# Token blocks of the later experts turned by VectorE instead of TensorE

## The chip, the cores and the metric

The kernel runs on one core of one Trainium2 chip. The metric is the device time of one execution in microseconds. A core has TensorE (matmuls, PE in the profile; its weight loads are PEld), VectorE (DVE), ScalarE (ACT), GpSimd (POOL), SyncE (SP, which here only issues DMAs) and 16 DMA engines. Each engine works through its own instructions in the order in which they were written; engines wait for each other by semaphores.

## The reference

A gated linear attention over 4 batches of 768 tokens with 8 heads of 48 gives 3072 rows `x` of 384 numbers. A router then picks one expert of eight per token, and each expert is a two-layer network:

```python
logits = x @ w_gate
e_idx = np.argmax(logits, axis=1)
...
for e in range(E):
    mask = e_idx == e
    h = np.maximum(x[mask] @ w1[e], 0.0)
    ye = h @ w2[e]
    out[mask] = gate_w[mask, None] * eom[mask, e, None] * ye
```

`w1[e]` is 384 by 1024 and `w2[e]` 1024 by 384, all in float32.

## The kernel before, in words

**Attention and sorting.** The first part of the program computes the attention and scatters every token's row into a DRAM buffer `xs_dram`. A row has 401 floats (1604 bytes): 384 of `x`, the number of the token, 8 logits and 8 output-gate logits. Each expert has its own stretch of that buffer, so after the scatter the tokens of one expert lie one behind the other.

**Experts.** The experts are then taken in order of their number of tokens; `s` counts them from 0 and has room for `CAPS` = 512, 448, 432, 416, 400, 400, 384, 376 tokens. Every product is made of three matmuls on a high and a low part of each operand (`xh`, `xl`, `w1h`, `w1l` and so on), which ScalarE and VectorE split: ScalarE rounds (`nc.scalar.copy`), VectorE subtracts. A stage of an expert has two halves. `mm1` (L750) multiplies `w1` with the tokens, eight blocks `f` of 128 rows of `h`, three chunks `c` of 128 features each, nine matmuls a block. `mm2` (L773, and `mm2_rows`, L787, for the last two experts, which have three row tiles) multiplies `w2` with `h`.

**Where the tokens come in.** `mm1` needs the tokens with their features on the partitions, but they lie in DRAM with one token to a row. `tokens_in` (L655) loads them in tiles `xg` of 128 tokens by 401 floats with one DMA. `x_in` (L721) turns them: for each chunk `c`, TensorE transposes three or four tiles of up to 128 tokens by 128 features into the PSUM tile `x_ps` (L711), then ScalarE casts `x_ps` to `xh` (L717) and VectorE subtracts it to get `xl` (L718).

**The order around it.** All orders are written out by hand. During the `mm2` half of stage `s`, a list `front` holds four splits of the next expert's `w1` (L636, L637) and three calls of `x_in(s + 1, c)` (L891 to L896). One entry is taken at each `f` of `mm2` (L907), or at every third step of `mm2_rows` (L900); the small operations that make the output gain of the next expert (`gain_ops`, L681) are taken in between. They are appended to each engine's instruction list behind the matmuls of that `f`. The last entry of `front` is `x_in(s + 1, 2)`; after it come the copies of the finished `y_ps` (`y_out`, L804), and then the first `mm1` of the next stage. TensorE also turns the finished output back (`put`, L811).

**The loads.** SP issues for each next expert four loads of `w1r` (L614), then the tokens (L658), then four of `w2r` (L626). The buffers of `w1r` and `w2r` are free again when a split has read them, so SP waits for the splits. Expert 0 is special: its tokens come in two parts into `first_x`, and are turned by TensorE in `x_early` and `x_late`.

Of the kernel before, what the change touches and what calls it, by code (L numbers as in the profile page):

```python
# [8 lines left out]
F32 = mybir.dt.float32  # L9
# [11 lines left out]
N, DM, E, F = B * S, H * D, 8, 1024  # L21
# [3 lines left out]
CAPS = (512, 448, 432, 416, 400, 400, 384, 376)  # L25
WARM = 22
TS = 128
NT = 4
SLOTS = NT * TS
WIDE = max(CAPS[1:])  # L30
# [4 lines left out]
KC = DM // 128  # L35
# [5 lines left out]
LG = DM + 1  # L41
RW = LG + 2 * E
RG = (4, 4, 4, 4, 2, 2, 2, 2)
XW = 2 * D + 2 * E
T_SCAT = 8
HELD = 256


class Consts:
# [66 lines left out]
class Routing:  # L116


    def __init__(self, pool):
        self.pend = pool.tile([128, NTC * NP], F32, name="pend")  # L120

        self.ohb = pool.tile([128, len(RG) + 1, 5, E], BF16, name="ohb")
        self.slot = pool.tile([128, NTC], I32, name="slot")
        self.top = pool.tile([128, E], F32, name="top")
        self.top_id = pool.tile([128, 1], I32, name="top_id")


def attention(ctx, tc, nc, k, kpool, rt, q01, k01, f01, q23, k23, f23, v, wg, xs_dram, r, ex):
# [205 lines left out]
    def scatter(n):  # L334

        for _ in range(min(n, len(sq))):
# [6 lines left out]

            for other in ex.apart + (ex.cleared if (t + 1) * C <= HELD else []):
                tc.declare_no_dep(i.ins, other.ins, reason="other slots")
# [77 lines left out]
    last = len(order) - 1  # L423
    pre_of = [prep(t) for t in range(len(order))]
    load(0, [("fqk", 0, 2), ("f", 2, 4), ("v", 0, 2), ("qk", 2, 4)])
    nc.sync.dma_start(out=turn[:, 0::2, 2 * D:XW], in_=wg[:, 0::2, 0:2 * E])
    for i in range(2):
        nc.sync.dma_start(out=turn[64 * i:64 * i + 64, 1::2, 2 * D:XW],
                          in_=wg[64 - 64 * i:128 - 64 * i, 1::2, 0:2 * E])
    load(0, [("v", 2, 4), ("fkqv", 4, 6)])  # L430
    load(1, [("fkqv", 0, 2), ("fkqv", 2, 4), ("fkqv", 4, 6)])
    for e in range(E):
        ex.clear(e)
# [144 lines left out]
class Experts:  # L578
# [4 lines left out]
    def __init__(self, tc, nc, k, r, raw, right, w1, w2, xs_dram, out, kp):  # L583
        self.tc, self.nc, self.k, self.r, self.raw, self.right, self.kp = tc, nc, k, r, raw, right, kp
        self.w1, self.w2, self.xs, self.out = w1, w2, xs_dram.rearrange("(e n) w -> e n w", e=E), out
        k.gain = kp.tile([TS, NT, E], F32, name="gain")
        k.dst = kp.tile([TS, NT, E], I32, name="dst")

        self.first = kp.tile([TS, NT, RW], F32, name="first_x")
        self.apart, self.cleared, self.number = [], [], {}  # L590
        self.wr, self.whl, self.todo, self.gq = {}, {}, [], []
        self.xg, self.xt, self.hs, self.ys, self.ysb = {}, {}, {}, {}, {}

    def open_early(self):
        pool = lambda name, bufs: self.right.enter_context(
# [14 lines left out]
    def load(self, s, number, rest=True):  # L610
        e = self.number[s] = self.nc.values_load(number, engines=[mybir.EngineType.SP], min_val=0, max_val=E - 1)
        for i in range(KF // 2):
            t = self.raw.tile([128, KC, 256], F32, name="w1r")
            self.nc.sync.dma_start(out=t, in_=self.w1[bass.ds(e, 1), :, 256 * i:256 * i + 256].rearrange(  # L614
                "o (c p) f -> p (o c) f", p=128))
            self.wr[1, s, i] = t
        if rest:
            self.load_rest(s)

    def load_rest(self, s):  # L620
        e = self.number[s]
        if s > 0:
            self.tokens_in(s, 0, len(self.rows(s)))
        for i in range(KF // 2):
            t = self.raw.tile([128, 2, DM], F32, name="w2r")
            self.nc.sync.dma_start(out=t, in_=self.w2[bass.ds(e, 1), 256 * i:256 * i + 256].rearrange(  # L626
                "o (c p) d -> p (o c) d", p=128))
            self.wr[2, s, i] = t
# [15 lines left out]
    def clear(self, e):  # L644

        if e == 0:
            self.empty = self.kp.tile([TS, RW], F32, name="empty")
            self.nc.gpsimd.memset(self.empty, 0.0)
            self.nc.gpsimd.memset(self.empty[:, DM:DM + 1], float(BIG))
        n = (SLOTS - HELD) // TS  # L650
        i = self.nc.sync.dma_start(out=self.xs[e, HELD:SLOTS].rearrange("(j p) w -> p j w", p=TS),
                                   in_=self.empty.unsqueeze(1).broadcast_to([TS, n, RW]))
        self.cleared.append(i)

    def tokens_in(self, s, j0, j1):  # L655
        early = s == 0 and j0 == 0
        t = self.first[:, j0:j1] if s == 0 else self.xp.tile([TS, NT, RW], F32, name="xg")
        i = self.nc.sync.dma_start(  # L658
            out=t[:, 0:j1 - j0, :],
            in_=self.xs[bass.ds(self.number[s], 1), j0 * TS:j1 * TS].rearrange("o (j p) w -> p (o j) w", p=TS))  # L660
        if early:

            for other in self.apart[T_TOP:]:
                self.tc.declare_no_dep(i.ins, other.ins, reason="other slots")
            self.apart.append(i)
        for j in range(j0, j1):
            self.xg[s, j] = (t[:, j - j0, :], min(TS, CAPS[s] - j * TS))
        if not early:
            self.meta = getattr(self, "meta", []) + [(s, 0, j1, t if s > 0 else self.first)]

    def gains(self):

# [8 lines left out]
    def gain_ops(self, s, j0, j1, t, d, up, dn, mx, sm, so):  # L681
        nc, k = self.nc, self.k
        tt, red, act = nc.vector.tensor_tensor, nc.vector.tensor_reduce, nc.scalar.activation
        sig, n = AF.Sigmoid, j1 - j0
        lg, og = t[:, 0:n, LG:LG + E], t[:, 0:n, LG + E:RW]
        mine = k.perm[:, s, :] if s > 0 else self.r.top
        return [
            lambda: nc.gpsimd.tensor_scalar(out=k.dst[:, j0:j1, s], in0=t[:, 0:n, DM], scalar1=0.0,
                                            scalar2=float(BIG), op0=ALU.max, op1=ALU.min),
            lambda: red(out=mx, in_=lg, axis=AX.X, op=ALU.max),  # L690
            lambda: tt(out=d, in0=lg, in1=mx.unsqueeze(2).broadcast_to([128, n, E]), op=ALU.subtract),

            lambda: (act(out=up, in_=d, func=sig), act(out=dn, in_=d, func=sig, scale=-1.0)),
            lambda: tt(out=d, in0=og, in1=mine.unsqueeze(1).broadcast_to([128, n, E]), op=ALU.mult),
            lambda: red(out=so, in_=d, axis=AX.X, op=ALU.add),
            lambda: act(out=so, in_=so, func=sig),
            lambda: nc.vector.reciprocal(out=dn, in_=dn),
            lambda: tt(out=up, in0=up, in1=dn, op=ALU.mult),
            lambda: red(out=sm, in_=up, axis=AX.X, op=ALU.add),
            lambda: nc.vector.tensor_scalar(out=sm, in0=sm, scalar1=1e-9, scalar2=None, op0=ALU.add),  # L700
            lambda: nc.vector.reciprocal(out=sm, in_=sm),
            lambda: tt(out=k.gain[:, j0:j1, s], in0=sm, in1=so, op=ALU.mult),
        ]
# [15 lines left out]
        return hi[:, 0:n], lo[:, 0:n]  # L719

    def x_in(self, s, c):  # L721
        ps = self.psx.tile([128, 512], F32, name="x_ps")
        for j, _ in self.rows(s):
            self.x_tr(s, c, ps, j, j * TS)
        self.xt[s, c] = self.x_split(self.xp, c, ps[:, 0:CAPS[s]], CAPS[s], WIDE, "x")

    def x_early(self):
        ps2 = self.psx.tile([128, 512], F32, name="x_ps")
# [189 lines left out]
def check(nc, k, r, pool, psum):  # L918
# [13 lines left out]
    def verdict():  # L932
        with nc.allow_low_precision(reason="a count of at most 17"):
# [7 lines left out]
        lambda: nc.vector.tensor_tensor(out=bad[:, 1:1 + E], in0=k.tokens, in1=k.caps, op=ALU.is_gt),  # L941
        lambda: nc.vector.tensor_scalar(out=bad[:, 1 + E:1 + 2 * E], in0=k.tokens, scalar1=float(HELD), scalar2=None,
                                        op0=ALU.is_lt),
# [189 lines left out]
```

## Time and profile before

| | |
|---|---|
| median of 3 runs | 380.4 us (378.98 to 382.08) |
| profiled execution | 383.17 us, its span 381.4 us |
| PE busy | 363.3 us, 95% of the span |
| DVE busy | 234.7 us, 62% |
| ACT busy | 197.7 us, 52% |
| POOL busy | 145.8 us, 38% |
| mean granted TensorE clock | 0.998 of full speed |

Times in the profile are microseconds from the start of the span. The attention takes the first 135 us or so; stages 0 to 7 follow, and the last matmul starts at 375.04. A busy share is an average over stages, so the rows below are read stage by stage.

### The profile page before, as it was taken

The page shows a single profiled execution, that of the slowest core. Times are in us where ns is not written, and L with a number is a line of the kernel's source. Part 1 is how long each engine was busy: PE and PEld are TensorE (multiplying, and loading weights), DVE is VectorE, ACT ScalarE, POOL GpSimd, SP SyncE. Part 2 cuts the span into 40 slices and gives each one's busy share as a digit, 9 for nine tenths or more (in the row PEclk, how much of TensorE's full clock was granted, in tenths as well). Part 3 has the DMA queues.
Part 4 walks back from the last instruction along what each step waited for, and adds up shares of the span by engine and source line. Part 5 has one row for each costly group of instructions (what it writes and reads, how often), then busy time and mean ns, then how long its engine had stood idle before and what let it go on. Part 6 is the DMA issues. An engine that isn't in the chain of part 4 may idle for free. (4 is left out here: it accounts for less than half of the span.)

```text
span 381.4 us, 8425 instructions
## 1 busy us (share of the span) xinstructions
PE 363.3 (95%) x3199; PEld 334.6 (88%) x3199; DVE 234.7 (62%) x482; ACT 197.7 (52%) x468; POOL 145.8 (38%) x176
## 2 busy tenths in 40 slices
PE   7899999998979999999999999999999999999993
PEld 2688978897868899989989999999999999999993
DVE  6988979897994773655644545463554554554610
ACT  3576856865745641536525634543652653753510
POOL 6686787997968670002201210310220220233012
PEclk9999999999999999999999999999999999999999
DMA  8999999999139327853434353445354354331001
GB/s 262 350 358 358 310 245 247 290 274 281 47 108 306 137 93 235 306 170 123 148 99 171 137 171 128 158 158 169 125 188 147 125 177 157 124 101 42 16 23 41
DMA packets 49315, 67.75 MB, mean 178 GB/s; under 512 B 3682, under 2 KB 43893, under 8 KB 49264
## 3 DMA queue, kind: packets, MB, share of 16 engines
q1 hardware_dynamic: 45952, 57.46, 49.6%
q0 software_dynamic: 3312, 9.65, 7.0%
q8 instruction: 27, 0.44, 0.5%
q14 instruction: 24, 0.20, 0.2%
HBM read 54.16 MB, written 13.39 MB: 177 GB/s over the span
## 5 line engine op out<-in xcount | busy, mean ns | idle before, releaser
L822 POOL DMA_INDIRECT out<-o,dst x30 | 30.2, 1007 | 188.3 <-ACT o L817 102.6
L766 DVE SCALAR_TENSOR_TENSOR hl<-h_ps,hh 128x256 fp32r<-128x256 f32 (+6 forms) x72 | 39.3, 546 | 53.1 <-ACT hh L765 52.3
L761 PE MATMUL h_ps<-xh,w1h 128*128 128x400 f32 (+6 forms) x192 | 67.3, 351 | 0.3 <-DVE hl L766 0.3
L761 PE MATMUL h_ps<-xh,w1l 128*128 128x400 f32 (+6 forms) x192 | 65.0, 338 | 0.0
L761 PE MATMUL h_ps<-xl,w1h 128*128 128x400 f32 (+6 forms) x192 | 64.9, 338 | 0.0
L765 ACT ACTIVATE hh<-h_ps 128x256 fp32r<-128x256 f32 (+6 forms) x72 | 34.8, 484 | 50.3 <-PE h_ps L761 48.6
L783 PE MATMUL y_ps<-hh,w2h 128*128 128x256 f32 (+4 forms) x168 | 57.7, 343 | 0.0
L783 PE MATMUL y_ps<-hl,w2h 128*128 128x256 f32 (+4 forms) x168 | 55.7, 332 | 0.0
L783 PE MATMUL y_ps<-hh,w2l 128*128 128x256 f32 (+4 forms) x168 | 55.6, 331 | 0.0
L718 DVE TENSOR_TENSOR xl<-x_ps,xh 128x400 fp32r<-128x400 f32 (+6 forms) x23 | 13.1, 568 | 41.8 <-ACT xh L717 38.5
L761 PEld LDWEIGHTS h_ps<-xh,w1h 128*128 128x128 f32 x192 | 36.1, 188 | 1.2 <-DVE hl L766 0.5
L761 PEld LDWEIGHTS h_ps<-xl,w1h 128*128 128x128 f32 x192 | 36.2, 188 | 0.4
L761 PEld LDWEIGHTS h_ps<-xh,w1l 128*128 128x128 f32 x192 | 36.0, 188 | 0.5
L717 ACT CAST xh<-x_ps 128x400 fp32r<-128x400 f32 (+6 forms) x23 | 11.3, 490 | 48.5 <-PE x_ps L711 42.4
L224 POOL TENSOR_TENSOR q_t<-q_t,p 128x512 f32<-128x512 f32 x24 | 30.6, 1276 | 9.6 <-DVE p L210 8.0
L637 DVE TENSOR_TENSOR w2l<-w2r,w2h 128x768 fp32r<-128x768 f32 x31 | 30.7, 991 | 4.2 <-ACT w2h L636 1.3
L783 PEld LDWEIGHTS y_ps<-hh,w2h 128*128 128x128 f32 x168 | 31.6, 188 | 1.0
L783 PEld LDWEIGHTS y_ps<-hl,w2h 128*128 128x128 f32 x168 | 31.6, 188 | 0.5
L783 PEld LDWEIGHTS y_ps<-hh,w2l 128*128 128x128 f32 x168 | 31.7, 188 | 0.4
L246 PE MATMUL a_ps<-q_t,k_t 64*128 64x128 f32 x384 | 28.3, 285 | 3.3 <-DVE k_t L221 2.7
L210 DVE TENSOR_TENSOR_SCAN p<-f_ps,start_p 128x511 f32<-128x511 f32 x22 | 28.0, 1273 | 3.9 <-ACT start_p L198 2.2
L323 PE MATMUL x_ps<-turn,xt 128*128 128x112 f32 x192 | 26.2, 280 | 3.8 <-ACT xt L317 3.6
(175 smaller groups left out, 773.1 us busy)
## 6 DMA issues: line engine op xcount, KB each, us to landing
w1r<-in_w SPq DMA_DIRECT2D x32, 384.0 KB
w2r<-in_w SPq DMA_DIRECT2D x32, 384.0 KB
xg<-xs_dram SPq DMA_DIRECT2D x5, 802.0 KB
xs_dram<-empty SPq DMA_DIRECT2D x8, 401.0 KB
f_t<-in_f SPq DMA_DIRECT2D x6, 512.0 KB
q_t<-in_q SPq DMA_DIRECT2D x6, 512.0 KB
k_t<-in_k SPq DMA_DIRECT2D x6, 512.0 KB
v_t<-in_v SPq DMA_DIRECT2D x6, 512.0 KB
```

Source lines behind the costliest of these rows:

```text
L210: nc.vector.tensor_tensor_scan(out=flat(d["p"])[:, 1:n], data0=flat(d["f"])[:, 0:n - 1], data1=sp[:, 1:n], initial=sp[:, 0:1], op0=ALU.mul ...
L224: nc.gpsimd.tensor_tensor(out=q_t[i][:, :, sl], in0=q_t[i][:, :, sl], in1=d["p"], op=ALU.mult)
L246: nc.tensor.matmul(aps[t][par][:, g, :], k_t[b % 2][r, g, sl], q_t[b % 2][r, g, sl], start=(g == 0), stop=(g == NP - 1))
L323: nc.tensor.matmul(xps[t][:, g, :], xt[t][:, g, :], turn[:, g, :], start=(g == 0), stop=(g == NP - 1))
L637: (eng or self.nc.vector).tensor_tensor(out=flat(lo), in0=flat(t), in1=flat(hi.bitcast(F32)), op=ALU.subtract)
L717: self.nc.scalar.copy(out=hi[:, 0:n], in_=ps)
L718: self.nc.vector.tensor_tensor(out=lo[:, 0:n], in0=ps, in1=hi.bitcast(F32)[:, 0:n], op=ALU.subtract)
L761: nc.tensor.matmul(ps[:, 0:n], a[:, c, cs], b, start=(i == 0), stop=(i == 3 * KC - 1))
L765: nc.scalar.activation(out=hi, in_=ps[:, 0:n], func=AF.Relu)
L766: nc.vector.scalar_tensor_tensor(out=lo, in0=ps[:, 0:n], scalar=0.0, in1=hi.bitcast(F32), op0=ALU.max, op1=ALU.subtract)
L783: self.nc.tensor.matmul(self.ys[d][:, c0:c0 + n], a[:, f % 2, ds], b, start=(f == 0 and i == 0 and part == 0), stop=(f == KF - 1 and i == ...
L822: self.nc.gpsimd.indirect_dma_start(out=self.out, out_offset=bass.IndirectOffsetOnAxis(ap=self.k.dst[0:n, j, s:s + 1], axis=0), in_=t[0:n] ...
```

## The change

For the experts 1 to 7 the tokens are no longer loaded as rows of 401 floats. Four DMAs each bring 96 of the 384 features of every token into one group of 32 partitions: token `32 a + t` lies on partition `32 b + t`, block `a`, where `b` is the group. A fifth DMA brings the token's number and the logits (`xm`). VectorE's transpose turns every 32 by 32 square of a tile in one instruction; with every third of the 96 features taken (`c::KC`), partition `32 b + i` then holds feature `96 b + 3 i + c`, which is `3 p + c` for partition `p`. The rows of `w1` are loaded in that same order. ScalarE's cast and VectorE's subtraction read the new SBUF tile `xc` in place of `x_ps`. Expert 0 is loaded and turned as before.

```diff
+SB = 32
+BW = DM // (128 // SB)
...
             self.nc.sync.dma_start(out=t, in_=self.w1[bass.ds(e, 1), :, 256 * i:256 * i + 256].rearrange(
-                "o (c p) f -> p (o c) f", p=128))
+                "o (p c) f -> p (o c) f" if s > 0 else "o (c p) f -> p (o c) f", p=128))
...
         if s > 0:
-            self.tokens_in(s, 0, len(self.rows(s)))
+            self.blocks_in(s)
...
+    def blocks_in(self, s):
+
+        e, nb, nt = self.number[s], -(-CAPS[s] // SB), len(self.rows(s))
+        t = self.xp.tile([128, SLOTS // SB, BW], F32, name="xb")
+        for b in range(128 // SB):
+            self.nc.sync.dma_start(
+                out=t[SB * b:SB * b + SB, 0:nb, :],
+                in_=self.xs[bass.ds(e, 1), 0:nb * SB, BW * b:BW * b + BW].rearrange("o (a t) w -> t (o a) w", t=SB))
+        m = self.xp.tile([TS, NT, RW - DM], F32, name="xm")
+        self.nc.sync.dma_start(
+            out=m[:, 0:nt, :],
+            in_=self.xs[bass.ds(e, 1), 0:nt * TS, DM:RW].rearrange("o (j p) w -> p (o j) w", p=TS))
+        self.xb[s] = t[:, 0:nb, :]
+        self.meta = getattr(self, "meta", []) + [(s, 0, nt, m)]
...
     def x_in(self, s, c):
-        ps = self.psx.tile([128, 512], F32, name="x_ps")
-        for j, _ in self.rows(s):
-            self.x_tr(s, c, ps, j, j * TS)
-        self.xt[s, c] = self.x_split(self.xp, c, ps[:, 0:CAPS[s]], CAPS[s], WIDE, "x")
+
+        t = self.xb[s]
+        n = t.shape[1] * SB
+        x = self.xp.tile([128, SLOTS], F32, name="xc")
+        self.nc.vector.transpose(out=x[:, 0:n].rearrange("p (a t) -> p a t", t=SB), in_=t[:, :, c::KC])
+        self.xt[s, c] = self.x_split(self.xp, c, x[:, 0:CAPS[s]], CAPS[s], WIDE, "x")
```

`gain_ops` reads the number and the logits from `xm` (or from the tail of `first_x` for expert 0) in place of `xg`.

## Rows read from the trace of the kernel before

**Rows 1.** The page's first part: busy time, share of the span and instructions of an engine.

```profile
PE 363.3 (95%) x3199; PEld 334.6 (88%) x3199; DVE 234.7 (62%) x482; ACT 197.7 (52%) x468; POOL 145.8 (38%) x176
```

**Rows 2.** Busy time by stretch: from and to, length, then busy time and number of instructions of PE, PEld, DVE, ACT and POOL, the granted TensorE clock, the mean busy share of the DMA engines, and GB/s. The first stretch lies in stage 0, the second is most of stage 1.

```profile
146.00:156.00 10.00, 10.00 (x84) 9.83 (x84) 4.33 (x13) 4.00 (x12) 0.79 (x2) 1.00 0.95 318
170.00:202.00 32.00, 32.00 (x168) 28.91 (x168) 16.60 (x37) 15.32 (x29) 4.49 (x5) 1.00 0.39 128
```

**Rows 3.** Everything that PE's matmuls waited for between 136 and 381 us: who waited for whom, us in total, times, the longest.

```profile
PE h_ps L761 <- DVE hl L766: 0.3, 1, 0.3
PE x_ps L711 <- DVE xl L718: 0.2, 1, 0.2
```

**Rows 4.** The instructions that read the tile `xg`: the transposes on PE, with their durations (least, median, greatest, ns), first and last start.

```profile
L711 PE MATMUL x_ps<-ident,xg x78: 230/272/327, 161.0 to 348.0; 128*128 128x128 f32 x60, 16*128 16x16 f32 x6, 64*128 64x64 f32 x3, 48*128 48x48 f32 x3
```

**Rows 5.** PE in order of time around one call of `x_in`, in the `mm2` half of stage 1: start, duration, instruction. Matmuls overlap, so starts are compared.

```profile
190.73 0.36 PE L783 MATMUL y_ps<-hh,w2l 128*128 128x448 f32 x1
190.93 0.36 PE L783 MATMUL y_ps<-hl,w2h 128*128 128x448 f32 x1
191.13 0.68 PE L711 MATMUL x_ps<-ident,xg 128*128 128x128 f32 x4
...
192.26 0.37 PE L783 MATMUL y_ps<-hl,w2h 128*128 128x448 f32 x1
```

**Rows 6.** The same around a call in stage 3.

```profile
253.49 0.35 PE L783 MATMUL y_ps<-hl,w2h 128*128 128x416 f32 x1
...
254.75 0.35 PE L783 MATMUL y_ps<-hl,w2h 128*128 128x416 f32 x1
254.94 0.35 PE L783 MATMUL y_ps<-hh,w2h 128*128 128x416 f32 x1
```

**Rows 7.** The same around a call in stage 6, where three tiles are turned.

```profile
340.38 0.34 PE L797 MATMUL y_ps<-w2h,hl 128*128 128x384 f32 x1
340.55 0.34 PE L797 MATMUL y_ps<-w2l,hh 128*128 128x384 f32 x1
340.73 0.48 PE L711 MATMUL x_ps<-ident,xg 128*128 128x128 f32 x3
...
341.41 0.34 PE L797 MATMUL y_ps<-w2l,hh 128*128 128x384 f32 x1
```

**Rows 8.** The same around the third call in stage 0.

```profile
165.36 0.28 PE L783 MATMUL y_ps<-hh,w2l 128*128 128x256 f32 x1
165.48 0.28 PE L783 MATMUL y_ps<-hl,w2h 128*128 128x256 f32 x1
165.98 0.75 PE L711 MATMUL x_ps<-ident,xg 128*128 128x128 f32 x4 [0.22 <-DVE xl L718]
...
167.00 0.28 PE L783 MATMUL y_ps<-hl,w2h 128*128 128x256 f32 x1
```

**Rows 9.** DVE's and ACT's groups by line and shape: count, busy us in total, mean ns of one, idle time before.

```profile
L718 DVE TENSOR_TENSOR xl<-x_ps,xh 128x448 fp32r<-128x448 f32 x3 | 1.9, 621 | 2.2 <-ACT xh L717 2.2
L718 DVE TENSOR_TENSOR xl<-x_ps,xh 128x256 fp32r<-128x256 f32 x2 | 0.8, 424 | 3.7 <-DMA w1r<-in_w 3.3 <-ACT xh L717 0.4
L210 DVE TENSOR_TENSOR_SCAN p<-f_ps,start_p 128x511 f32<-128x511 f32 x22 | 28.0, 1273 | 3.9 <-ACT start_p L198 2.2 <-ACT xt L317 0.9 <-ACT f_ps L205 0.7
L717 ACT CAST xh<-x_ps 128x448 fp32r<-128x448 f32 x3 | 1.6, 535 | 3.1 <-PE x_ps L711 3.1
```

**Rows 10.** DVE in order of time through the `mm2` half of stage 0, which has the tokens of stage 1 to turn, and ACT's last split there.

```profile
160.18 0.96 DVE L637 TENSOR_TENSOR w1l<-w1r,w1h 128x768 fp32r<-128x768 f32 x1 [0.30 <-ACT w1h L636]
161.06 0.18 DVE L690 TENSOR_REDUCE g_mx<-xg 128x4 f32<-128x32 f32 x1
...
163.26 0.82 ACT L636 CAST w1h<-w1r 128x768 fp32r<-128x768 f32 x1
...
167.33 0.62 DVE L718 TENSOR_TENSOR xl<-x_ps,xh 128x448 fp32r<-128x448 f32 x1 [1.15 <-ACT xh L717]
```

**Rows 11.** PE's first matmul of the next stage's `mm1`: after stage 0, after stage 1, and after stage 6.

```profile
169.94 0.37 PE L761 MATMUL h_ps<-xh,w1h 128*128 128x448 f32 x1
202.50 0.36 PE L761 MATMUL h_ps<-xh,w1h 128*128 128x432 f32 x1
350.18 0.34 PE L761 MATMUL h_ps<-xh,w1h 128*128 128x376 f32 x1
```

**Rows 12.** DVE in stage 1: the second of four splits of `w1`. Then ACT's copy of the second output tile of stage 6.

```profile
188.31 0.95 DVE L637 TENSOR_TENSOR w1l<-w1r,w1h 128x768 fp32r<-128x768 f32 x1
345.87 0.58 ACT L801 ACTIVATE o<-y_ps,gain 128x384 f32<-128x384 f32 x1 [0.64 <-PE y_ps L797]
```

**Rows 13.** The tokens' way in, in order of time: SP's issue for stage 1 and the instruction on POOL that waited for its landing; SP's issue for stage 3 and the first transposes of those tokens.

```profile
148.62 0.37 SPq L658 DMA_DIRECT2D xg<-xs_dram  x1
155.47 0.88 POOL L688 TENSOR_SCALAR dst<-xg 128x4 int32<-128x4 f32 x1 [8.93 <-DMA xg<-xs_dram]
199.26 0.37 SPq L658 DMA_DIRECT2D xg<-xs_dram  x1
223.01 0.66 PE L711 MATMUL x_ps<-ident,xg 128*128 128x128 f32 x4
```

**Rows 14.** The page's third part: a DMA queue with its packets, MB, and the time of the packets as a share of 16 engines' span.

```profile
q1 hardware_dynamic: 45952, 57.46, 49.6%
q0 software_dynamic: 3312, 9.65, 7.0%
```

More of the change, by code (lines that the diff above doesn't have):

```diff
@@ L591, in __init__ @@
         self.wr, self.whl, self.todo, self.gq = {}, {}, [], []
-        self.xg, self.xt, self.hs, self.ys, self.ysb = {}, {}, {}, {}, {}
+        self.xg, self.xb, self.xt, self.hs, self.ys, self.ysb = {}, {}, {}, {}, {}, {}
     def open_early(self):
@@ L655, in tokens_in @@
     def tokens_in(self, s, j0, j1):
-        early = s == 0 and j0 == 0
-        t = self.first[:, j0:j1] if s == 0 else self.xp.tile([TS, NT, RW], F32, name="xg")
+        early = j0 == 0
+        t = self.first[:, j0:j1]
         i = self.nc.sync.dma_start(
-            out=t[:, 0:j1 - j0, :],
-            in_=self.xs[bass.ds(self.number[s], 1), j0 * TS:j1 * TS].rearrange("o (j p) w -> p (o j) w", p=TS))
+            out=t, in_=self.xs[bass.ds(self.number[s], 1), j0 * TS:j1 * TS].rearrange("o (j p) w -> p (o j) w", p=TS))
         if early:
@@ L668, in tokens_in @@
         if not early:
-            self.meta = getattr(self, "meta", []) + [(s, 0, j1, t if s > 0 else self.first)]
+            self.meta = getattr(self, "meta", []) + [(s, 0, j1, self.first[:, :, DM:RW])]
+    def blocks_in(self, s):
[11 more added lines that the diff above has]
+        self.meta = getattr(self, "meta", []) + [(s, 0, nt, m)]
     def gains(self):
@@ L684, in gain_ops @@
         sig, n = AF.Sigmoid, j1 - j0
-        lg, og = t[:, 0:n, LG:LG + E], t[:, 0:n, LG + E:RW]
+        lg, og = t[:, 0:n, 1:1 + E], t[:, 0:n, 1 + E:1 + 2 * E]
         mine = k.perm[:, s, :] if s > 0 else self.r.top
         return [
-            lambda: nc.gpsimd.tensor_scalar(out=k.dst[:, j0:j1, s], in0=t[:, 0:n, DM], scalar1=0.0,
+            lambda: nc.gpsimd.tensor_scalar(out=k.dst[:, j0:j1, s], in0=t[:, 0:n, 0], scalar1=0.0,
                                             scalar2=float(BIG), op0=ALU.max, op1=ALU.min),
```

## The prediction

> **What bounds the kernel now.** I began with the page's first part: PE is busy for 95% of the span, and no other engine for more than 62% [rows 1]. A busy share doesn't yet say that PE sets the pace, so I went on to busy time by stretch. In stage 1 PE is busy for all 32.00 us, while DVE has 16.60 and ACT 15.32 [rows 2]. The list of waits then says the same from the other side: between 136 and 381 us the matmuls waited 0.5 us in all for anybody [rows 3]. So from about 139 us to the end the time is the sum of what PE's queue holds, and an instruction taken out of that queue is worth what it costs there, as long as nothing else comes late in its place.
>
> **What is taken out of PE's queue.** 78 transposes [rows 4], in 21 calls of `x_in`: 15 calls of four tiles (experts 1 to 5), 6 of three (experts 6 and 7). Their durations overlap with the matmuls around them, so I price a call by starts: from the last matmul before it to the third after it, less three ordinary steps. In stage 1: 192.26 - 190.93 = 1.33, less 3 x 0.20, is 0.73 [rows 5]. In stage 3: 1.26 less 3 x 0.19 is 0.69 [rows 6]. With three tiles: 0.86 less 3 x 0.175 is 0.33 [rows 7]. In stage 0 the matmuls are 0.12 apart, and the third call, which also waits for DVE to free `x_ps`, costs 1.52 - 0.36 = 1.16 [rows 8]; for the other two I take 0.72. Sum: 12 x 0.71 + 6 x 0.33 + (2 x 0.72 + 1.16) = 8.5 + 2.0 + 2.6 = **13.1 us**.
>
> **What VectorE gets.** 21 transposes, each of up to 448 elements on 128 partitions. No row shows such an instruction. The nearest ones by size: a subtraction of 448 takes 0.62, one of 256 takes 0.42, a scan of 511 takes 1.27 [rows 9]. The least I allow is 0.42 (a pass at almost two elements in the time of one), the most 1.27 (a pass as slow as the scan's); I take 0.62, since the transpose too reads and writes each element once, as the subtraction does and the scan, which carries a result along, does not. Cast and subtraction now read SBUF; I leave them at 0.54 and 0.62 [rows 9]. DVE's busy time grows by 3 x 0.62 = 1.9 us in a stage of 30, from half busy. That is no bound. What counts is the order: transpose, cast on ACT, subtraction follow each other, some 1.9 us a chunk with the handovers, and DVE stands while ACT casts. What is queued behind on DVE is the next split of `w1` and the small gain operations, and `mm1` of the next stage waits for the third chunk.
>
> Stage 1 first. DVE no longer waits for PE's place in the list, so it can run on from the second split, which ends at 189.3 [rows 12]: three chunks 5.6, two splits 1.9, some ten small operations of 0.2 bring it to 198.8. `mm1` now starts at 202.50 [rows 11] less 2.2 = 200.3, and needs the third chunk six matmuls later, at 201.5. **2.7 us to spare.** In stage 6 ACT must first copy the second output tile, which ends PE's work on it: 345.87 [rows 12] less two calls' 0.66, with the copy 345.8; then a split (0.82 and 0.96), a small operation and a chunk of 1.7 give 349.5, against 350.18 [rows 11] - 1.0 + 1.05 = 350.2. 0.7 to spare.
>
> Stage 0 is the tight one, since its `mm2` has only the 256 late columns of expert 0 left to do. DVE's split ends at 161.14 and the first gain operation at 161.24 [rows 10]. First chunk ready at 163.1; ACT's last split, before at 163.26 [rows 10], at about 163.5, DVE's part of it done at 165.3; two small operations; second chunk ready at 167.5; a small one; third chunk's `xh` at 168.8, `xl` at 169.5. PE would get to `mm1` at 169.94 [rows 11] - 2.6 = 167.3 and to the third chunk's `xl` at 168.7. It waits **0.8 us**. With a transpose of 1.27 all three chunks shift it, and the wait is 2.8; with 0.42 it is 0.2. Elsewhere both ends are covered by the time to spare.
>
> A rule speaks against this part. The Trainium skill, VectorE: DVE Perf Modes, section "The three transpose paths", gives 311 ns for 128 by 128 on VectorE, turned only in squares of 32, and its section "Rules for kernel authors" sends a 128 by 128 transpose to TensorE where PSUM will do as destination. At its price 3.5 such tiles would be an estimate of 1.09 us a chunk, and the sum 1.4 us worse, 369.5; no row here shows it, and what the rule leaves out is that here PE has no time to give.
>
> **The loads.** One DMA of 512 pieces of 1604 bytes becomes 14 x 128 = 1792 pieces of 384 bytes and 512 of 68. Three things follow. SP issues four more DMAs a stage, at 0.37 each [rows 13]; SP mostly waits for splits there, so I cost it at nothing, with at most 1.5 us of later `w2r` loads if that cover is gone. On the engines, the loads' queue spent 49.6% of 16 x 381.4 us on 45952 packets [rows 14], 66 ns for 1250 bytes on average. By bytes, the old load was 512 x 85 / 16 = 2.7 us of all engines; the new one is 2.4 if time goes by bytes and 2304 x 66 / 16 = 9.5 if it goes by packets. So the tokens land between 0.3 us earlier and 6.8 later. Who waits for that? In stages 1 to 6 nobody: tokens issued at 199.26 are turned from 223.01 [rows 13]. In stage 0 the DMA engines are busy for 95% [rows 2]; issued at 148.62, the tokens were there at 155.5 [rows 13]. DVE wants them at 161.1 [rows 10]. The worst end, 162.2, adds 1.1 us. I take a landing near 158, which costs nothing: a piece of 384 bytes is nearer to the byte end than to that of 1250. The order of `w1`'s rows changes neither the size nor the number of pieces; I cost it at nothing.
>
> **Sum.** 13.1 - 0.8 = 12.3 us less. The profiled execution took 383.17, its span 381.4 with 1.8 around it, 2.8 above the median; the sum turns 383.17 into 370.9 and the median of 380.4 into **368.1**. With both unknown costs at their upper ends the gain is 13.1 - 2.8 - 1.1 = 9.2, 371.2; at the lower ends 12.9, 367.5.
>
> **Rivals.**
> *The chain on DVE and ACT comes in front of PE in every stage* (chance 0.12). If a chunk takes 3.0 us and not 1.9, by a transpose of 1.7 or slow handovers, stage 0 waits 0.8 + 3.3 = 4.1, each of the later ones some 0.5: 13.1 - 7.1 = 6, 374.4. For it: DVE's work is strictly in order and was never asked for this. Against: no DVE row of that size is so slow, and half of DVE's time is free.
> *The small pieces hold up stage 0 until the kernel is slower* (0.06). With P ns a packet the tokens land 2304 P / 16 after the `w1` loads, against 2.7 now; the 5.7 us to spare and then the whole 12.3 are used up at 20.7 us, P = 144 ns. At P = 180 the result is 385.6. Against it: that is over twice the mean of 66, and above the 129 ns that a packet of the other queue takes at 2.9 kB [rows 14]. For it: no row has pieces this small, and the engines are full there. The Trainium skill, DMA: Bandwidth & Descriptors, section "Specifications", puts the least size for line rate at 512 bytes, with a read-modify-write below; that names no price, and no row here shows it.
> *The change doesn't pay out* (0.08): PE's busy matmuls are modelled, and if the pace were set by something that the waits don't show, the freed places would be filled with idle time, 379 to 381. Against it: the steps of 0.20 resume right behind each call [rows 5].
>
> **How the numbers follow.** The forecast (0.74) has its own range, 366 to 371.2, which allows for 1.5 us of scatter between runs. The first rival lies mostly within 374.5. So 365.5 to 374.5 leaves out the other two and the tail of the first, under 2 in 10. A measurement of this kernel can tell about 1% from no change, 376.6 to 384.2. Faster: 0.74 + 0.12 = 0.86; within 1%: 0.08; slower: 0.06.
>
> **What the changed kernel's profile would show.** No transposes of `xg` on PE, and in the `mm2` halves steps of 0.18 to 0.20 without a break. DVE transposes of about 0.6, early in each `mm2` half. The stage boundaries after 202 us 2 us closer together, the last two by 1. One wait of PE near 168 for DVE's `xl`, under 1 us. The tokens of stage 1 landing before 161. I am wrong if PE waits at every boundary, if a transpose takes over 1.3 us, or if POOL or DVE waits for `xm` past 162.

## The result, and the profile after

The changed kernel takes **367.84 us** (median of 4 runs, 367.22 to 368.0); the kernel before took 379.87 in the 4 runs that it was compared with. The ratio is 0.9672, with a 95% interval of 0.9627 to 0.9717. The forecast was 368.1.

| | before | after |
|---|---|---|
| profiled execution, its span | 383.17, 381.4 | 368.0, 366.3 |
| PE busy | 363.3, 95% | 351.9, 96% |
| DVE busy | 234.7, 62% | 245.9, 67% |
| packets of the loads' queue | 45952 | 58048 |

The two profiled spans are 15.1 us apart, which is more than the change brought. To compare runs I use a **stretch**: from the first matmul of `mm2` on the 256 late columns of expert 0 (the first place behind which the two programs differ on PE) to the last matmul. Here are its ends in the kernel before, from PE in order of time:

```profile
158.84 0.28 PE L783 MATMUL y_ps<-hh,w2h 128*128 128x256 f32 x1
...
375.04 0.34 PE L797 MATMUL y_ps<-w2l,hh 128*120 128x384 f32 x1
```

And in the kernel after, with the beginnings of stage 1's two halves between them:

```profile
155.57 0.28 PE L801 MATMUL y_ps<-hh,w2h 128*128 128x256 f32 x1
...
164.02 0.37 PE L779 MATMUL h_ps<-xh,w1h 128*128 128x448 f32 x1
...
181.09 0.36 PE L801 MATMUL y_ps<-hh,w2h 128*128 128x448 f32 x1
...
359.95 0.34 PE L815 MATMUL y_ps<-w2l,hh 128*120 128x384 f32 x1
```

The stretch went from 375.04 - 158.84 = 216.20 us to 359.95 - 155.57 = 204.38: **11.82 less**. The other 3.27 lie ahead of it, in the attention, and aren't the change's: the kernel before with nothing but the order of `w1`'s rows changed began its stretch at 155.4, the changed kernel, in another run, at 157.7. Cut at the halves of each stage, in the same way:

| half | before | after | |
|---|---|---|---|
| `mm2` of stage 0 | 11.10 | 8.45 | -2.65 |
| `mm1` of stage 1 | 15.79 | 17.07 | +1.28 |
| `mm2` of stage 1 | 16.77 | 14.54 | -2.23 |
| `mm2` of stage 2 | 16.04 | 13.92 | -2.12 |
| `mm2` of stage 3 | 15.53 | 13.44 | -2.09 |
| `mm2` of stage 4 | 15.20 | 13.15 | -2.05 |
| `mm2` of stage 5 | 14.13 | 13.15 | -0.98 |
| `mm2` of stage 6 | 13.69 | 12.72 | -0.97 |
| the other halves | 97.95 | 97.94 | 0 |

Every half that lost its transposes became shorter, 13.09 us in all; one half became longer. Its place is in the list of what PE's matmuls waited for between 130 and 366 us (who for whom, us in total, times, the longest), which answers to [rows 3]:

```profile
PE h_ps L779 <- DVE hl L784: 0.7, 2, 0.3
PE h_ps L779 <- ACT xh L733: 0.5, 1, 0.5
PE h_ps L779 <- DVE xl L734: 0.2, 1, 0.2
```

The two waits of the first line lie ahead of the stretch. The last two lines are new. PE in order of time shows them at the start of stage 1:

```profile
165.03 0.36 PE L779 MATMUL h_ps<-xh,w1l 128*128 128x448 f32 x1
165.89 0.47 PE L779 MATMUL h_ps<-xh,w1h 128*128 128x448 f32 x1 [0.50 <-ACT xh L733]
166.55 0.47 PE L779 MATMUL h_ps<-xl,w1h 128*128 128x448 f32 x1 [0.19 <-DVE xl L734]
166.85 0.36 PE L779 MATMUL h_ps<-xh,w1l 128*128 128x448 f32 x1
```

Starts that should be 0.20 apart are 0.86 and 0.66 apart. The matmul at 165.89 is the first that reads the third chunk; it waits for ScalarE's cast, the next for VectorE's subtraction. On VectorE this answers to [rows 10]:

```profile
157.79 0.18 DVE L706 TENSOR_REDUCE g_mx<-xm 128x4 f32<-128x32 f32 x1
157.89 0.77 DVE L742 STREAM_TRANSPOSE xc<-xb 128x448 f32<-128x448 f32 x1
159.29 0.62 DVE L734 TENSOR_TENSOR xl<-xc,xh 128x448 fp32r<-128x448 f32 x1 [0.63 <-ACT xh L733]
159.84 0.18 DVE L707 TENSOR_TENSOR g_d<-xm,g_mx 128x32 f32<-128x32 f32 x1
161.16 0.96 DVE L639 TENSOR_TENSOR w1l<-w1r,w1h 128x768 fp32r<-128x768 f32 x1 [1.14 <-ACT w1h L638]
...
162.36 0.77 DVE L742 STREAM_TRANSPOSE xc<-xb 128x448 f32<-128x448 f32 x1
163.76 0.63 DVE L734 TENSOR_TENSOR xl<-xc,xh 128x448 fp32r<-128x448 f32 x1 [0.63 <-ACT xh L733]
164.30 0.35 DVE L713 RECIPROCAL g_dn<-g_dn 128x32 f32<-128x32 f32 x1
164.56 0.68 DVE L742 STREAM_TRANSPOSE xc<-xb 128x448 f32<-128x448 f32 x1
165.87 0.62 DVE L734 TENSOR_TENSOR xl<-xc,xh 128x448 fp32r<-128x448 f32 x1 [0.63 <-ACT xh L733]
```

VectorE waits for nothing from PE here, and it isn't busy all the time: in brackets is the time in which it stood while ScalarE cast a chunk or rounded a split. The third subtraction ends at 166.49, 2.5 us after PE got to `mm1`.

### The profile page after: what moved, and what is told of

Same layout as the page of the kernel before. It is cut to its first block, busy times and chain, and to the rows that moved or that the text cites. A ratio compares the mean times of both kernels' runs of the same rounds, so it can differ in the third digit from the quotient of the medians.

```text
span 366.3 us, 8386 instructions
## 1 busy us (share of the span) xinstructions
PE 351.9 (96%) x3121; PEld 327.0 (89%) x3121; DVE 245.9 (67%) x503; ACT 198.1 (54%) x468; POOL 146.2 (40%) x176
## 3 DMA queue, kind: packets, MB, share of 16 engines
q1 hardware_dynamic: 58048, 56.82, 56.1%
## 5 line engine op out<-in xcount | busy, mean ns | idle before, releaser
L840 POOL DMA_INDIRECT out<-o,dst x30 | 31.0, 1033 | 172.9 <-ACT o L835 87.5
L801 PE MATMUL y_ps<-hh,w2h 128*128 128x256 f32 (+4 forms) x168 | 55.8, 332 | 0.0
L639 DVE TENSOR_TENSOR w1l<-w1r,w1h 128x768 fp32r<-128x768 f32 x28 | 26.9, 960 | 4.0 <-ACT w1h L638 2.5
L248 PEld LDWEIGHTS a_ps<-q_t,k_t 64*128 64x128 f32 x384 | 23.6, 187 | 6.5 <-POOL k_t L223 2.5
L223 POOL TENSOR_TENSOR k_t<-k_t,i 128x512 f32<-128x512 f32 x21 | 27.0, 1285 | 4.2 <-DVE i L219 2.7
```

The costliest lines, as they stand in the source:

```text
L223: eng.tensor_tensor(out=k_t[i][:, :, sl], in0=k_t[i][:, :, sl], in1=d["i"], op=ALU.mult)
L248: nc.tensor.matmul(aps[t][par][:, g, :], k_t[b % 2][r, g, sl], q_t[b % 2][r, g, sl], start=(g == 0), stop=(g == NP - 1))
L639: (eng or self.nc.vector).tensor_tensor(out=flat(lo), in0=flat(t), in1=flat(hi.bitcast(F32)), op=ALU.subtract)
L801: self.nc.tensor.matmul(self.ys[d][:, c0:c0 + n], a[:, f % 2, ds], b, start=(f == 0 and i == 0 and part == 0), stop=(f == KF - 1 and i == ...
L840: self.nc.gpsimd.indirect_dma_start(out=self.out, out_offset=bass.IndirectOffsetOnAxis(ap=self.k.dst[0:n, j, s:s + 1], axis=0), in_=t[0:n] ...
```

## The experiments

All of them are read by the stretch: 216.20 before, 204.38 after.

**The transposes put back into PE's list.** Loads, VectorE's part and the layout stay as changed; nobody uses what PE turns.

```diff
         self.nc.vector.transpose(out=x[:, 0:n].rearrange("p (a t) -> p a t", t=SB), in_=t[:, :, c::KC])
+        ps = self.psx.tile([128, 512], F32, name="x_ps")
+        for j, m in self.rows(s):
+            self.nc.tensor.transpose(out=ps[:, j * TS:j * TS + m], in_=self.first[0:m, 0, c * 128:(c + 1) * 128],
+                                     identity=self.k.ident[0:m, 0:m])
```

> The changed kernel, with the 78 transposes put back into TensorE's list at their old places; they read a resident tile, write x_ps, and nobody uses the result. Loads, VectorE's transposes, casts and subtractions stay as changed. Compared is the stretch from the first matmul of mm2 on expert 0's late columns to the last matmul of the kernel: 216.2 us before, 204.4 after. Theory (the gain is the places freed in TensorE's queue): 204.4 + 13.1, and the 1.3 us wait at the start of stage 1 vanishes because TensorE gets there 2.2 later, so 216.2, and a time of 379 to 381. Rival (loads, layout or the freed x_ps buffer brought the gain): 204 to 210, 368 to 373.

Measured: 379.73 us, against 379.58 for the kernel before on the same chip; the stretch is 215.79. PE around one call, as in [rows 5]:

```profile
187.89 0.36 PE L805 MATMUL y_ps<-hl,w2h 128*128 128x448 f32 x1
188.09 0.68 PE L745 MATMUL x_ps<-ident,first_x 128*128 128x128 f32 x4
...
189.22 0.37 PE L805 MATMUL y_ps<-hl,w2h 128*128 128x448 f32 x1
```

189.22 - 187.89 = 1.33, less 0.60: 0.73 a call again, although nothing waits for the result. The wait in stage 1 is gone: `mm1` took 15.78, as before the change. The 0.4 us short of 216.2 are in stage 0's `mm2` (10.72 against 11.10), where the third call no longer waits for VectorE to free `x_ps`. So the gain is the places in PE's queue, and neither the loads nor the layout has a part in it.

**Only the order of `w1`'s rows,** in the kernel before:

```diff
-                "o (c p) f -> p (o c) f", p=128))
+                "o (p c) f -> p (o c) f" if s > 0 else "o (c p) f -> p (o c) f", p=128))
```

> The kernel before, with only the order of w1's rows changed for experts 1 to 7; the tokens' features are not put into that order, so that product pairs other rows than it should. Theory (same number and size of pieces): the stretch stays at 216.2 within 0.2, the time at 379 to 382, no wait for w1. Rival (the new order makes the w1 loads slower or faster): matmuls wait for a split of w1, or the stretch moves by over 0.5.

Measured: the stretch is 216.19, the time 379.46. The order costs nothing and brings nothing.

**Every chunk turned twice,** the second time into a scratch tile behind the first:

```diff
+        y = self.xp.tile([128, SLOTS], F32, name="xd", bufs=1)
+        self.nc.vector.transpose(out=y[:, 0:n].rearrange("p (a t) -> p a t", t=SB), in_=t[:, :, c::KC])
```

> The changed kernel, each of VectorE's 21 transposes done twice, the second into a scratch tile. Same stretch. Theory (only stage 0 has no time to spare): the wait for the tokens at the start of stage 1 grows from 1.3 to about 3.5 us (three transposes of 0.75 more), the other boundaries lose nothing, 206.6 in all. Rival (the chain on VectorE and ScalarE stands close in front of TensorE everywhere): each of the six later boundaries loses 0.7 to 1.5 as well, 211 to 216.

Measured: 368.16, the stretch is 204.36. **Both theories missed**: 21 more transposes of 0.7 us cost nothing at all. VectorE in order of time shows where they went:

```profile
157.98 0.78 DVE L742 STREAM_TRANSPOSE xc<-xb 128x448 f32<-128x448 f32 x1
158.68 0.75 DVE L744 STREAM_TRANSPOSE xd<-xb 128x448 f32<-128x448 f32 x1
159.39 0.63 DVE L734 TENSOR_TENSOR xl<-xc,xh 128x448 fp32r<-128x448 f32 x1
```

The subtraction starts 1.41 us after the first transpose, as it did without the second (159.29 - 157.89 = 1.40). VectorE stood for 0.63 us there anyway, waiting for the cast, and the extra transpose fills that hole. That was an experiment on idle time, not on the chain, so the extra one was put in front.

**The same ahead of the real transpose, once and twice.**

```diff
+        y = self.xp.tile([128, SLOTS], F32, name="xd", bufs=1)
+        for _ in range(1):
+            self.nc.vector.transpose(out=y[:, 0:n].rearrange("p (a t) -> p a t", t=SB), in_=t[:, :, c::KC])
         self.nc.vector.transpose(out=x[:, 0:n].rearrange("p (a t) -> p a t", t=SB), in_=t[:, :, c::KC])
```

> The changed kernel, with one more transpose into a scratch tile ahead of each of the 21, not behind it. Behind it the second one cost nothing, which we put down to the 0.6 us in which VectorE stands while ScalarE casts. Same stretch, 204.4 in the changed kernel. Theory (VectorE, ScalarE and VectorE in turn are a chain, and only stage 0 has no time to spare): three times 0.73 more at the start of stage 1, nothing elsewhere, since the third chunk's subtraction ended 2.8, 3.3, 2.9, 2.6, 2.5 and 0.65 us ahead of the matmul that needs it at the six later boundaries: 206.6. Rival (VectorE has room for a second transpose wherever it stands): 204.4 to 205.

> The same with two more transposes ahead of each of the 21, which is as if one took 2.2 us. Theory: 4.4 us more at the start of stage 1; the five four-tile boundaries after it lose 4.2 less their time to spare, 1.4, 0.9, 1.3, 1.6 and 1.7, and the last one 0.7: 204.4 + 4.4 + 6.9 + 0.7 = 216.4, so no faster than before the change. Rival (as above): under 207.

(The second run has `range(2)`.) Measured: 375.42 us with a stretch of 210.28, and 388.29 with 222.81. The chain is real. With one more transpose the five boundaries behind stage 1 lost nothing; with two they lost 1.37, 1.02, 1.40, 1.66 and 1.13 (forecast 1.4, 0.9, 1.3, 1.6, 1.7), so four bore out their time to spare and the fifth lost less. But stage 1's `mm1` lost 4.52 and 6.86 us, where 2.2 and 4.4 were expected, and the last boundary 1.27 and 5.0, where 0 and 0.7 were. Two things had been left out.

The first is the granted clock. Busy time by stretch of the run with one more, columns as in [rows 2]:

```profile
166.00:168.00 2.00, 1.53 (x6) 0.52 (x4) 1.37 (x4) 0.67 (x2) 0.00 (x0) 1.00 1.00 285
168.00:169.00 1.00, 0.02 (x1) 0.00 (x0) 0.81 (x2) 0.15 (x1) 0.00 (x0) 0.98 1.27 204
169.00:170.00 1.00, 0.54 (x1) 0.29 (x1) 0.56 (x2) 1.00 (x3) 0.00 (x0) 0.50 1.30 199
170.00:172.00 2.00, 2.00 (x6) 1.71 (x6) 1.62 (x8) 1.11 (x3) 0.00 (x0) 0.50 0.57 57
174.00:176.00 2.00, 2.00 (x9) 1.72 (x7) 0.62 (x1) 1.13 (x2) 0.00 (x0) 0.55 0.53 165
176.00:180.00 4.00, 4.00 (x24) 3.68 (x23) 1.58 (x2) 2.21 (x5) 1.08 (x1) 1.00 0.18 65
```

From 166 to 169 PE was busy for 1.55 of 3 us. From about 169 the granted clock, which had been 1.00, was 0.50, the lower of its two levels (1.2 GHz and not 2.4), until about 175.8 (0.55 from 174 to 176 is 1.8 us at 0.50 and 0.2 at 1.00). From 170 on PE is busy all the time and does six matmuls in 2 us, where it does thirteen at full clock (168 to 170 in the changed kernel). PE in order of time there:

```profile
165.65 0.37 PE L782 MATMUL h_ps<-xh,w1h 128*128 128x448 f32 x1
...
169.47 0.74 PE L782 MATMUL h_ps<-xh,w1h 128*128 128x448 f32 x1 [1.44 <-ACT xh L733]
170.12 0.74 PE L782 MATMUL h_ps<-xl,w1h 128*128 128x448 f32 x1
...
171.04 0.57 PE L782 MATMUL h_ps<-xh,w1h 128*128 128x448 f32 x1
171.41 0.57 PE L782 MATMUL h_ps<-xl,w1h 128*128 128x448 f32 x1
```

The matmul that reads the third chunk's `xl` starts 170.12 - 165.65 = 4.47 us after the first of `mm1`; in the changed kernel it was 166.55 - 164.02 = 2.53. So the waits are 1.94 us longer, near the 2.2 expected. The other 2.6 of the 4.52 lie behind them, in steps of 0.37 in place of 0.20: some 15 lose 0.17 each. In the run with two more it is 4.42 and 2.4. In the changed kernel the wait is shorter (PE busy for 1.50 of the 2 us from 164, and 1.81 of the next two) and the clock stays at 1.00.

The second is that at the last boundary the extra transposes of all three chunks count; the expectations had counted those of the third alone. In the changed kernel the third `xl` is ready 0.65 us ahead there. Three more transposes of 0.66 are 2.0, less 0.65 is 1.3, and 1.27 were lost, at a clock of 1.00. PE there, in the run with one more:

```profile
343.04 0.43 PE L782 MATMUL h_ps<-xh,w1h 128*128 128x376 f32 x1 [0.59 <-ACT xh L733]
343.62 0.44 PE L782 MATMUL h_ps<-xl,w1h 128*128 128x376 f32 x1
```

With two more transposes that matmul for `xl` comes 3.35 us later than in the changed kernel (4.0 less 0.65), and the other 1.65 of the 5.0 go with a granted clock of 0.50 from 356 to 358.

**The tokens loaded twice.** Four equal loads into a scratch tile go ahead of the real ones:

```diff
-        for b in range(128 // SB):
+        u = self.xp.tile([128, SLOTS // SB, BW], F32, name="xe", bufs=1)
+        for b in range(256 // SB):
             self.nc.sync.dma_start(
-                out=t[SB * b:SB * b + SB, 0:nb, :],
-                in_=self.xs[bass.ds(e, 1), 0:nb * SB, BW * b:BW * b + BW].rearrange("o (a t) w -> t (o a) w", t=SB))
+                out=(u if b < 4 else t)[SB * (b % 4):SB * (b % 4) + SB, 0:nb, :],
+                in_=self.xs[bass.ds(e, 1), 0:nb * SB, BW * (b % 4):BW * (b % 4) + BW].rearrange("o (a t) w -> t (o a) w", t=SB))
```

> The changed kernel, the four block loads of an expert preceded by four equal ones into a scratch tile, so 1792 more pieces of 384 bytes for expert 1. Same stretch. In the changed kernel the last part of expert 1's tokens landed by 155.1 and VectorE first wanted it at 157.8. Theory (a piece costs about 36 ns of one of 16 engines, from the growth of the queue's packet time): landing 4 us later, so about 1.3 us past the need, 205.7, and nothing at the later experts. Rival A (time by bytes, 20 ns): 2.3 us later, still hidden, 204.4. Rival B (as dear as an average packet, 66 ns): 7.4 later, 209.

Measured: 369.77, the stretch is 204.86, and nothing lost at the later experts. In this run the stretch begins at 157.22, 1.65 later than in the profile above. VectorE, then POOL, when the tokens come:

```profile
159.85 0.19 DVE L707 TENSOR_REDUCE g_mx<-xm 128x4 f32<-128x32 f32 x1 [0.34 <-DMA xm<-xs_dram]
160.00 0.25 POOL L705 TENSOR_SCALAR dst<-xm 128x4 int32<-128x4 f32 x1 [14.72 <-DMA xm<-xs_dram]
```

VectorE now waits for the tokens, 0.34 us, which is most of what the stretch lost (0.48). They came 2.8 us after the stretch's beginning, against 0.5 before it in the changed kernel (POOL started at 155.10 there), so 1792 more pieces took some 3 us, between rival A and the theory. The price of a piece, from the third part of the two pages: the queue's share grew from 56.1% of 366.3 to 64.7% of 368.1 us, times 16 engines, 523 us for 12096 packets, 11648 of them pieces of 384 bytes: **43 ns each**. That price includes what the other packets lost by them: the packet records of the trace have 34.5 ns on average for a piece of 384 bytes in the changed kernel, and 37.6 in this run.

**The tokens first.** In stage 0 the three chunks are turned ahead of the last two splits of `w1`:

```diff
-                front.insert(2 * c + 2 if s > 0 else 2 * c + 1, lambda c=c: self.x_in(s + 1, c))
+                front.insert(2 * c + 2 if s > 0 else c, lambda c=c: self.x_in(s + 1, c))
```

> The changed kernel, with one order altered: in stage 0 the three chunks of expert 1's tokens are turned first and the last two splits of w1 follow them. Theory (the 1.3 us wait at the start of stage 1 is the order on VectorE and ScalarE, not the landing of the loads): the third chunk is ready some 2 us earlier, the wait goes, nothing is late in its place (the last split is first used 7 us into stage 1), so the stretch is 203.1 and the time 1.3 us below the changed kernel's, about 366.5. Rival (the tokens land too late for it): VectorE waits for the loads or for its own transposes, and the stretch stays within 0.3 of 204.4.

> The changed kernel as it is, for comparison with the reordered one on the same chip and for the scatter of the part ahead of the change. Theory: 367 to 368.5, the stretch 204.4 within 0.2, the start of that stretch anywhere from 155 to 159, since nothing ahead of it was changed. Rival (the attention part too became faster by the change): the stretch starts at 155.6 again, and every run with the changed loads starts there.

Measured: 366.59 us (366.36 to 366.9, 5 runs) with a stretch of 203.10, and 368.22 (367.3 to 370.1, 6 runs) with 204.35 for the changed kernel as it is; against the kernel before the ratios are 0.9636 (0.9608 to 0.9664) and 0.9678 (0.965 to 0.9705). `mm1` of stage 1 is back at 15.79, and PE's two waits in the stretch are gone. VectorE's third subtraction, then PE's first two matmuls that read the third chunk:

```profile
162.03 0.63 DVE L734 TENSOR_TENSOR xl<-xc,xh 128x448 fp32r<-128x448 f32 x1 [0.63 <-ACT xh L733]
165.21 0.36 PE L779 MATMUL h_ps<-xh,w1h 128*128 128x448 f32 x1
165.41 0.36 PE L779 MATMUL h_ps<-xl,w1h 128*128 128x448 f32 x1
```

The subtraction now ends at 162.7, ahead of `mm1`, and the two matmuls are an ordinary step of 0.20 apart. So the wait was the order on VectorE and ScalarE and not the landing, and this order beats both kernels: the slowest run with it is below the fastest of the changed kernel. The intervals of the two ratios overlap; that the step is 1.25 us is shown by the stretch, in which halves that an edit doesn't touch agree to about 0.1 from run to run. The profiled run of the changed kernel as it is began its stretch at 157.7, so the attention's start isn't part of the change.

## Why the prediction was right

**The bound and the 13.1 us.** The halves that lost transposes became 13.09 us shorter (2.65 in stage 0 for 2.6 forecast, 2.23 in stage 1 for 3 x 0.73), and putting the transposes back restored the time. Pricing a call by starts, 0.73, 0.69 and 0.33, was what made this close: by the median duration of 0.272 the 78 transposes would have been 21.2 us [rows 4]. The gain was forecast as 12.3 us and was 11.82 by the stretch; that 367.84 nevertheless lies below 368.1 is scatter between runs, the kernel before being at 379.87 here and at 380.4 in the forecast.

**The wait at stage 1** was foreseen in its place and its cause, but sized at 0.8 us; it was 1.28, and that is the 0.5 us by which the gain fell short. Two terms were too small. The first is the price of a chunk. From VectorE's and ScalarE's groups by shape (columns as in [rows 9]):

```profile
L742 DVE STREAM_TRANSPOSE xc<-xb 128x448 f32<-128x448 f32 x6 | 4.5, 749 | 0.0
L742 DVE STREAM_TRANSPOSE xc<-xb 128x384 f32<-128x384 f32 x6 | 4.0, 668 | 0.0
L733 ACT CAST xh<-xc 128x448 fp32r<-128x448 f32 x3 | 1.7, 566 | 5.3 <-DVE xc L742 5.3
```

The transpose takes 0.75 where I took 0.62 from the subtraction, the cast 0.57 where I left it at 0.54, and a chunk about 2.0 where I had 1.9 with the handovers. Counted from the stretch's beginning the third subtraction was to end at 169.5 - 158.84 = 10.66 and ended at 166.49 - 155.57 = 10.92: 0.26 later. The second term lies on PE, behind the wait, where I had counted nothing: its matmul starts 0.06 after the subtraction's end, and the step behind it is 0.30 (166.55 to 166.85) in place of 0.20; with a few hundredths in the steps that follow this makes the other 0.2. The sign of a single wait, for `xl` and under 1 us, was not met: there are two waits, the first for ScalarE's `xh`.

The estimate of 1.09 us a chunk, worked out from the Trainium skill, VectorE: DVE Perf Modes, "The three transpose paths", was too high: the trace has 0.75, in one instruction. The advice in the Trainium skill, VectorE: DVE Perf Modes, "Rules for kernel authors", to turn 128 by 128 on TensorE does not hold here, where PE is the bound: turning on VectorE freed 13.09 us of PE, and the wait took 1.28 of them back.

**The time to spare** at the later boundaries was worked out as 2.7 us for stage 1 and 0.7 for stage 6. In the changed kernel the third subtraction ended 2.8 and 0.65 us ahead of the matmul that reads it. For stage 1 the working held too: with two more transposes ahead of each chunk that boundary lost 1.37, where 1.4 was expected. For stage 6 the number is right, but by luck in part. I began that chain at ScalarE's copy of the second output tile, which waited 0.64 us for PE before [rows 12] and behind which only one chunk follows. In the changed kernel it waits for nobody; it stands in ScalarE's list behind the second chunk's cast, which waits for VectorE:

```profile
330.95 0.51 ACT L733 CAST xh<-xc 128x376 fp32r<-128x376 f32 x1 [2.07 <-DVE xc L742]
331.36 0.58 ACT L819 ACTIVATE o<-y_ps,gain 128x384 f32<-128x384 f32 x1
```

So the path ran through all three chunks on VectorE, as the 1.27 us lost with one more transpose in each show.

**The loads.** I had the tokens land 2.5 us later than before; seen from the stretch's beginning it was 2.9 (155.10 against 155.57, and before 155.47 against 158.84), 2.7 us ahead of VectorE's first use. A small piece costs 35 to 43 ns, between the 20 and the 66 that bounded it. By the byte that is 0.09 to 0.11 ns, about twice the 0.05 of an average packet; here it costs nothing, because nobody waits. The Trainium skill, DMA: Bandwidth & Descriptors, "Specifications", says that pieces under 512 bytes miss line rate; the trace agrees. SP's issues at 0.37 each were priced too low: the four block loads took SP 3.43 us in stage 0, with the DMA engines busy for 94%, the fifth load 1.71, and the four of the next expert 2.38. What makes an issue longer wasn't tried, and nothing waited for it.

**The rivals.** The chain in front of PE in every stage came true only with two more transposes a chunk. That tells how near it was: with 2.2 us in place of 0.75 the change would have made the kernel slower, 388.29 against 383.07 for the kernel before on the same chip. The small pieces were far from the 144 ns at which they would have used up the gain. And the freed places were not filled with idle time: seven halves are shorter by what the calls cost.

## What to carry to other kernels

Where one engine's queue is full from end to end, price an instruction by what it moves the starts of its neighbours, not by its duration, and look for an engine that is half idle to take it. The engine that takes it no longer keeps step with the old order: work out, at each place where its result is needed, how much time is to spare, and turn the entries of the list round where there is none. Follow the chain back through all its steps, and not only to a wait that the change itself may take away. To test whether a chain is tight, lengthen it ahead of the step in question; behind it an extra instruction may fall into a hole.

## What was not expected of the hardware

I had priced a wait of PE at its own length. In the run with one transpose more ahead of each chunk, waits 1.94 us longer cost 4.52: after 3 us in which PE was busy for 1.55, the granted clock went from 1.00 to 0.50 and stayed there until about 175.8, almost 7 us. The Trainium skill, TensorE: Matmul & The Clock Gate, "Part 1", says that the clock follows how busy PE has been; the run agrees. In the changed kernel the wait of 1.28 us left the clock at 1.00, and so did the 1.27 us lost at the last boundary of that same run.

A transpose on VectorE of a tile read with every third element took 0.75 us for 448 elements where a subtraction of as many takes 0.62; where the 0.13 come from, the stride, the squares or the instruction itself, wasn't tried.
